# Hash-bucket attention followed by an RWKV channel mix: v centred for all pairs, mix vectors loaded as rows, dummy matmuls in the prologue, one pair's row copies on another queue, and a new instruction order

## The chip, the core and the metric

The kernel runs on one NeuronCore of one Trainium2 chip. The metric is the device time of one launch in microseconds, lower is better. Before the change three runs gave 252.12, 250.82 and 248.18 us, so the median is 250.82 us.

The core has engines that each work through a list of instructions of their own in order: PE (matrix multiply), ACT (activation), DVE (vector), POOL (a slower vector engine) and SP, which here only issues DMAs. ACT issues a few DMAs too. An instruction that waits for a semaphore holds back everything behind it on its engine.

## What is computed

```python
B, H, S, D = 4, 8, 768, 64                      # q, k, v: [B, H, S, D]; proj: [D, 6]
q_bits = (q @ proj) > 0;  k_bits = (k @ proj) > 0       # six sign bits
mask   = all six bits of a query equal those of a key
scores = where(mask, q @ k.T / sqrt(D), -1e9)
attn   = softmax(scores);  o = attn @ v                 # per head
x      = o with heads side by side                      # [B, S, 512]
xk     = x_prev + mu_k * (x - x_prev);  xr the same with mu_r
out    = sigmoid(xr @ w_r) * (relu(xk @ w_k)**2 @ w_v)  # w_k: 512x1024
```

## The kernel before

Two heads make a pair; there are 16 pairs, four to a batch. Each pair `n` goes through these steps.

1. **Load and split.** `ldq` loads q and k (`nat`), `ldv` loads v (`vn`), 384 KB each, on SP's queue. `hi` (L556, or L618 for the first two pairs) rounds four times the value to fp16, `lo` (L559, L621) takes the rest, so that the two fp16 halves stand beside each other in `nh`.
2. **Transpose.** `tr` (L563) is a DMA transpose of `nh` to `a`. For pairs 0 and 1 PE does it instead (L635) and ACT or DVE copies it out of PSUM (`evt`, L639).
3. **Hash bits.** `bits` (L587) multiplies the projection with `a`. A result has six rows for each piece of 256 positions; `GROUPS` says over how many column tiles of PE these are spread (4 unless it is given there, 2 for pairs 1 to 3). `bx` (L591) turns signs into plus or minus a constant, and `row` (L599) copies these rows by DMA behind the 64 rows of the values, so that one matmul gives score plus match bonus. Pair 0 has these rows written directly (L657, L663, L665).
4. **Scores.** Nine steps a pair of 1024 columns: PE L708 into PSUM (three slots of two banks), then ACT L712 takes the exponential into `pt`.
5. **v.** For pairs below `NUC = 8`, v is used as it is: L501 copies it to bf16 with a column of ones (`va`), `vsum` (L509, L512, L515) adds it up, and one extra matmul for each output tile (L736, weights `tiny` = 1e-12) puts in the term that stands for a row without any match. From pair 8 on v is centred: the mean comes from two small matmuls (L528, L529), two instructions of L534 write v minus its mean, and the mean goes into `mc` (L541) and the boundary column (L772).
6. **Output of attention.** PE L741 multiplies `pt` with `va`; DVE takes the reciprocal of the sum (L751, or L753 and L754 where v is centred) and scales (L758, `ob`). The result is turned into `xt` by PE (L794) or by a DMA transpose (L768).
7. **Mix.** L829, L837, L841 make `xk` and `xr` in bf16. L837 multiplies by `muk` or `mur`, and adds `mc` where v is centred.

After the fourth pair of a batch the channel mix of the batch is released: L859 (w_k), `relu` on ACT L864 or DVE L866, the square L869, then L884 (w_r) with a tanh L887, L896 (w_v), L903 and the store L907. So matmuls of batch b fill PE while pairs of batch b+1 wait for ACT.

The order is not found at run time. Each piece of work is recorded with its engine, its dependences and an estimated duration; `ORDER`, a list of 1386 numbers, gives the order in which the recorded pieces are handed to the engines, and `WHERE` gives the engine of each piece that can run on several. A PSUM bank is chosen in that order too. The engines then run their lists in order, and semaphores do the rest. So an entry of `ORDER` decides what stands ahead of what on PE, ACT, DVE, POOL and in SP's DMA queue.

Around this: seven matmuls on zeros (L390) run first, the identity matrices and the weights of `bits` are made on POOL, and `muk` and `mur` are loaded on ACT's queue so that each of 128 partitions gets four values of four bytes:

```python
nc.scalar.dma_start(out=t, in_=src.rearrange("(c p) -> p c", p=P))     # L422, 512 elements of 4 bytes
nc.sync.dma_start(out=a_t[sa][D : D + NB, ...], in_=bx_t[sx][...])     # L599, two or four per pair
```

Of the kernel before, what the change touches and what calls it, by code (L numbers as in the profile page):

```python
# [9 lines left out]
FP32 = mybir.dt.float32  # L10
# [25 lines left out]
def R(kind, n):  # L36
# [223 lines left out]
def kernel(  # L260
# [24 lines left out]
    STEP = 1024  # L285
    NSTEP = 2 * NSC * S // STEP
    NPB = H // 2
    NPAIRS = B * NPB

    NWARM = 7  # L290
    GROUPS = {1: 2, 2: 2, 3: 2}
    HALVED = (2, 3)
    NFOLD = 3
    FW = S // NFOLD
    NUC = 8
    V_GQ = ()
    MERGED = ()
# [667 lines left out]
```

## Time and profile before

| | |
|---|---|
| three runs | 252.12, 250.82, 248.18 us (median 250.82) |
| span of the profiled execution, first to last instruction | 251.3 us |
| PE busy | 236.9 us (94%), 2609 matmuls |
| weight loads of PE | 147.6 us (59%) |
| DVE busy | 195.4 us (78%), 471 instructions |
| ACT busy | 179.1 us (71%), 225 instructions |
| POOL busy | 27.9 us (11%), 73 instructions |
| DMA | 44.56 MB, 177 GB/s on average |

The profile gives no other time for the profiled execution than its span; the span is 0.5 us above the median of the three runs. PE's busy time is modelled for pipelined matmuls, so a busy share of 94% is not 94% of what PE can do. The kernel has four stretches: a prologue up to about 18 us in which PE has little to do; the first batch's attention up to about 60 us; attention and channel mix together up to about 195 us; and the last channel mix up to the end.

### The profile page before, as it was taken

What the parts mean: (1) busy time and instruction counts of PE and PEld (TensorE: products, weight loads), DVE (VectorE), ACT (ScalarE), POOL (GpSimd) and SP (SyncE); (2) the same over time, 40 slices, a digit from 0 to 9 for tenths busy, and PEclk for the clock granted to TensorE, in tenths of its full rate; (3) what the DMA queues carried; (4) which work ended last, traced back from release to release, by engine and by line L of the source; (5) the groups of instructions that cost most, each with busy time, mean ns of one, the idle gap of its engine ahead of it and who ended that gap; (6) DMA issues with size and microseconds to landing.
All of it is one profiled execution on the core that took longest, in us unless ns stands there. A gap on an engine that the chain in (4) does not pass through costs nothing.

```text
span 251.3 us, 6510 instructions
## 1 busy us (share of the span) xinstructions
PE 236.9 (94%) x2609; PEld 147.6 (59%) x2609; DVE 195.4 (78%) x471; ACT 179.1 (71%) x225; POOL 27.9 (11%) x73
## 2 busy tenths in 40 slices
PE   6886799999799998999999999999999999999993
PEld 2444578876566655666467566655865654545442
DVE  3795679889788889898998999899787878376322
ACT  5596689999799978996878899988787223332220
POOL 5002240541302031100001100100000000000000
PEclk9799799999999999999999999999999999999998
DMA  6999999999989999999999996793231030022223
GB/s 187 308 178 251 220 215 191 267 249 189 213 292 241 204 293 292 273 201 269 184 333 186 184 185 158 210 230 57 90 64 44 0 128 28 13 83 86 83 85 125
DMA packets 75194, 44.56 MB, mean 177 GB/s; under 512 B 55524, under 2 KB 70172, under 8 KB 75164
## 3 DMA queue, kind: packets, MB, share of 16 engines
q1 hardware_dynamic: 74028, 44.15, 72.8%
q8 instruction: 20, 0.33, 0.6%
q10 hardware_dynamic: 1136, 0.01, 0.3%
q14 instruction: 10, 0.08, 0.1%
HBM read 24.12 MB, written 6.29 MB: 121 GB/s over the span
## 4 chain that ended last, share of the span: by engine, by line
PE 75%; DMA 11%; DVE 8%; SPq 3%; ACT 1%; issue 1%; DVEq 0%
PE ps_all L708 19%; PE ps_all L896 17%; PE ps_all L859 13%; PE ps_all L741 12%; PE ps_all L884 8%; DMA nat<-in_k_dram 5%; PE ps_all L587 4%; DMA nat<-in_q_dram 3%; DMA a<-bx 2%; DMA os<-in_moe_w_k_dram 1%; DVE nh L559 1%; DVE nh L556 1%; PE ps_all L736 1%; ACT pt L712 1%; PE ps_all L794 1%
## 5 line engine op out<-in xcount | busy, mean ns | idle before, releaser
L712 ACT ACTIVATE pt<-ps_all 128x1024 bf16<-128x1024 f32 x144 | 138.8, 1040 | 21.1 <-PE ps_all L708 19.8
L708 PE MATMUL ps_all<-a 128*128 128x512 f16 (+3 forms) x408 | 80.6, 318 | 5.1 <-DMA a<-bx 3.9
L708 PEld LDWEIGHTS <-a 128*128 128x128 f16 x408 | 35.3, 98 | 26.7 <-DMA a<-bx 4.7
L859 PE MATMUL ps_all<-xk,wk 128*128 128x384 bf16 x256 | 49.0, 326 | 0.9 <-DVE kr L866 0.9
L896 PE MATMUL ps_all<-wv,k 128*128 128x512 bf16 (+1 forms) x200 | 45.9, 370 | 0.6 <-DVE os L903 0.6
L741 PEld LDWEIGHTS <-pt 128*128 128x128 bf16 x1152 | 42.1, 98 | 6.9 <-issue 1.1
L741 PE MATMUL ps_all<-va,pt 128*128 128x65 bf16 x1152 | 43.9, 194 | 0.0
L859 PEld LDWEIGHTS <-wk 128*128 128x128 bf16 x256 | 24.5, 98 | 17.6 <-issue 1.6
L896 PEld LDWEIGHTS <-k 128*128 128x128 bf16 x200 | 19.4, 98 | 20.6 <-issue 0.7
L864 ACT ACTIVATE kr<-ps_all 128x384 bf16<-128x384 f32 x33 | 15.8, 493 | 19.2 <-DVE k L869 12.7
L887 ACT ACTIVATE rs<-ps_all 128x512 f32<-128x512 f32 x24 | 14.2, 603 | 20.9 <-PE ps_all L884 19.0
L559 DVE SCALAR_TENSOR_TENSOR nh<-nat,nh 128x768 f16<-128x768 f32 x28 | 27.3, 976 | 1.1 <-ACT nh L554 0.6
L903 DVE SCALAR_TENSOR_TENSOR os<-rs,ps_all 128x512 f32<-128x512 f32 (+1 forms) x25 | 16.5, 662 | 14.7 <-PE ps_all L896 9.9
L869 DVE TENSOR_TENSOR k<-kr 128x384 bf16<-128x384 bf16 x64 | 21.5, 350 | 3.7 <-ACT kr L864 3.5
L884 PE MATMUL ps_all<-wr,xr 128*128 128x512 bf16 x96 | 23.8, 379 | 0.0
L866 DVE TENSOR_SCALAR kr<-ps_all 128x384 bf16<-128x384 f32 x31 | 17.1, 555 | 8.3 <-PE ps_all L859 6.6
L758 DVE TENSOR_TENSOR ob<-ps_all,rc 128x384 bf16<-128x384 f32 (+1 forms) x36 | 18.3, 511 | 1.0
L884 PEld LDWEIGHTS <-xr 128*128 128x128 bf16 x96 | 9.0, 98 | 10.0 <-ACT kr L864 0.3
L587 PE MATMUL ps_all<-a,p0g 128*32 128x256 f16 (+1 forms) x180 | 13.4, 276 | 1.3 <-DMA a<-nh 1.3
L556 DVE TENSOR_SCALAR nh<-nat 128x768 f16<-128x768 f32 x22 | 12.3, 557 | 3.0 <-DMA nat<-in_q_dram 2.5
L587 PE MATMUL ps_all<-a,p1g 128*32 128x256 f16 (+1 forms) x180 | 12.9, 273 | 0.0
L841 DVE TENSOR_TENSOR xr<-tm,xt 128x768 bf16<-128x768 f16 (+1 forms) x18 | 9.4, 520 | 0.4
(94 smaller groups left out, 187.4 us busy)
## 6 DMA issues: line engine op xcount, KB each, us to landing
vn<-in_v_dram SPq DMA_DIRECT2D x16, 384.0 KB
out_dram<-os SPq DMA_DIRECT2D x23, 256.0 KB
nat<-in_k_dram SPq DMA_DIRECT2D x15, 384.0 KB
nat<-in_q_dram SPq DMA_DIRECT2D x15, 384.0 KB
wst<-in_moe_w_k_dram SPq DMA_DIRECT2D x2, 512.0 KB
wst<-in_moe_w_r_dram SPq DMA_DIRECT2D x2, 512.0 KB
wst<-in_moe_w_v_dram SPq DMA_DIRECT2D x2, 512.0 KB
a<-bx SPq DMA_DIRECT2D x48, 9.0 KB
```

The costliest lines, as they stand in the source:

```text
L559: nc.vector.scalar_tensor_tensor(out=nh[:, :, D:P], in0=nat.rearrange("p j (c d) -> p (j c) d", d=D), scalar=QS, in1=nh[:, :, 0:D], op0=AL ...
L587: nc.tensor.matmul(ps[g_ * wid : (g_ + 1) * wid, 0:FW], w_[:, m_ - 1 - x : m_ - 1 - x + wid], a_t[sa][:, i, x % NFOLD * FW : (x % NFOLD + ...
L708: nc.tensor.matmul(ps[:, lo - s * STEP : hi - s * STEP], side_a["k"][sa][:, j, jc * P : (jc + 1) * P], side_a["q"][sa][:, j, q0 : q0 + hi ...
L712: nc.scalar.activation(out=pt_t[sp][:, s * STEP : (s + 1) * STEP], in_=ps_t[plan.slot[nm]], func=AF.Exp, bias=EBIAS, scale=ESC)
L741: nc.tensor.matmul(oo[:, (ic - c0) * 65 : (ic - c0) * 65 + 65], pt_t[sp][:, o : o + P], va_t[sa][:, j, jc, 0 : D + 1], start=(not uc and i ...
L758: nc.vector.tensor_tensor(out=ob_t[so][:, c0:c1, j * D : (j + 1) * D], in0=oo[:, :, 0:D], in1=rc_t[sr][:, 1, c0:c1].unsqueeze(2).to_broadc ...
L859: nc.tensor.matmul(ps[:, 0:HALF], wk_sb[:, d, fc * P : (fc + 1) * P], xk_t[mx[d]][:, h * HALF : (h + 1) * HALF], start=(d == 0), stop=(d = ...
L866: nc.vector.tensor_scalar(out=kr_t[sk], in0=sm(nm)[:, 0:HALF], scalar1=0.5 ** 0.5, scalar2=0.0, op0=ALU.mult, op1=ALU.max)
L869: nc.vector.tensor_tensor(out=k2_t[s2][:, h * HALF : (h + 1) * HALF], in0=kr_t[sk], in1=kr_t[sk], op=ALU.mult)
L884: nc.tensor.matmul(sm(nr), xr_t[mx[d]][:, c * P : (c + 1) * P], wr_sb[:, d, :], start=(d == 0), stop=(d == NDC - 1))
L896: nc.tensor.matmul(sm(nv)[:, lo:hi], k2_t[(b * NFC + fc) % NK2][:, c * P : (c + 1) * P], wv_sb[:, fc, lo:hi], start=(fc == 0), stop=(fc == ...
L903: nc.vector.scalar_tensor_tensor(out=os_t[so][:, lo:hi], in0=rs_t[s1][:, lo:hi], scalar=1.0, in1=sm(nv)[:, lo:hi], op0=ALU.add, op1=ALU.mult)
```

## The change

- `NUC` goes from 8 to 0: v is centred for all pairs. For pairs 0 to 7 the extra matmuls of L736 and the copies of L501 are gone; the two small matmuls for the mean, the instructions of L534, L541 and L772 and the additional L753 come in.
- `mu_k` and `mu_r` are loaded as eight rows of 128 values, turned by one fp32 matmul with an 8x8 identity (made on POOL), and lowered by one in a single DVE instruction.
- Six more dummy matmuls (`keep`) on the same zeros, placed by `ORDER`; the seven of before are placed anew too.
- The two row copies of pair 1 are issued by ACT (`ROW_ACT`), not by SP.
- `GROUPS` keeps the value 2 for pair 1 alone: `bits` of pairs 2 and 3 are spread over four column tiles, with four row copies each in place of two.
- `ORDER` (now 1429 numbers) and `WHERE` are new throughout.

The core of the diff, without the two tables:

```diff
     NWARM = 7
-    GROUPS = {1: 2, 2: 2, 3: 2}
+    NWARM2 = 6
+    GROUPS = {1: 2}
...
-    NUC = 8
+    NUC = 0
...
-    ROW_ACT = ()
+    ROW_ACT = ((1, 0), (1, 1))
...
-    muk = buf([P, NDC], FP32, "muk")
-    mur = buf([P, NDC], FP32, "mur")
+    mu8 = tm_t[1].bitcast(FP32)[0 : 2 * NDC, 0:P]
+    id8 = buf([2 * NDC, 2 * NDC], FP32, "id8")
+    mu_t = buf([P, 2 * NDC], FP32, "mu")
+    muk, mur = mu_t[:, 0:NDC], mu_t[:, NDC : 2 * NDC]
...
+    for i in range(NWARM2):
+        add("PE", 0.2155, -7.5 + 0.15 * i, lambda: nc.tensor.matmul(sm("warm2"), wz[:, 0:P], wz, start=True, stop=True),
+            r=["wz"], w=["warm2"], ..., name="keep")
...
-    for t, src, key in ((muk, moe_mu_k, "muk"), (mur, moe_mu_r, "mur")):
-        def f_mu(t=t, src=src):
-            with nc.allow_non_contiguous_dma(reason="512 values"):
-                nc.scalar.dma_start(out=t, in_=src.rearrange("(c p) -> p c", p=P))
-        add("ACT", 1.05, -19.0, f_mu, w=[key], ...)
-        add("DVE", 0.17, 1.3, lambda t=t: nc.vector.tensor_scalar(
-            out=t, in0=t, scalar1=-1.0, scalar2=None, op0=ALU.add), r=[key], w=[key])
+    add("POOL", 0.3, -2.2, lambda: make_identity(nc, id8), w=["id8"], name="id8")
+    for i_, src in enumerate((moe_mu_k, moe_mu_r)):
+        add("ACT", 0.42, -19.0, lambda i_=i_, src=src: nc.scalar.dma_start(out=mu8[i_ * NDC : (i_ + 1) * NDC, :], in_=src.rearrange("(c p) -> c p", p=P)),
+            w=[("mu8", i_)], ...)
+    add("PE", 0.12, 1.0, lambda: nc.tensor.matmul(sm("mu")[:, 0 : 2 * NDC], mu8, id8, start=True, stop=True), ...)
+    add("DVE", 0.08, 1.3, lambda: nc.vector.tensor_scalar(out=mu_t, in0=sm("mu")[:, 0 : 2 * NDC], scalar1=-1.0, scalar2=None, op0=ALU.add), ...)
...
-            def row(g_=g_):
-                nc.sync.dma_start(out=a_t[sa][D : D + NB, ...], in_=bx_t[sx][...])
-            add("SP", 0.72, R("row", n) + 0.01 * g_, row, r=[("bx", sx)], ...
+            on = "ACT" if (n, g_) in ROW_ACT else "SP"
+            def row(g_=g_, e=nc.scalar if on == "ACT" else nc.sync):
+                e.dma_start(out=a_t[sa][D : D + NB, ...], in_=bx_t[sx][...])
+            add(on, 0.75, R("row", n) + 0.01 * g_, row, r=[("bx", sx)], ...
```

What the two tables change, counted from the instruction lists of the two programs: of 36 `hi`, DVE has 18 (27 before), ACT 15 (9) and POOL 3 (none); of 64 `relu`, DVE has 24 (31) and ACT 40 (33); of the 16 first sums of `vsum`, DVE has 6 (15) and POOL 10 (1); of the ten weight casts, DVE has 2 (4), ACT 1 (2) and POOL 7 (4). On ACT the two loads of the mix vectors and that of the projection come first, and the activation table is loaded behind them. On SP the loads of v for pairs 1 and 0 come right behind the loads of pair 2. On DVE, `hi` and `lo` of pair 2 stand behind the bits of pair 0's first half (L665) and not ahead of them.

More of the change, by code (lines that the diff above doesn't have):

```diff
@@ L389 @@
     for i in range(NWARM):
-        add("PE", 0.43, -20.0 + 0.1 * i, lambda: nc.tensor.matmul(sm("warm"), wz[:, 0:P], wz, start=True, stop=True),
-            r=["wz"], w=["warm"], take=("sm", "warm", 0) if i == 0 else None, give=["warm"] if i == NWARM - 1 else [])
+        add("PE", 0.2155, -20.0 + 0.1 * i, lambda: nc.tensor.matmul(sm("warm"), wz[:, 0:P], wz, start=True, stop=True),
+            r=["wz"], w=["warm"], take=("sm", "warm", 0) if i == 0 else None, give=["warm"] if i == NWARM - 1 else [], name="warm")
+    for i in range(NWARM2):
+        add("PE", 0.2155, -7.5 + 0.15 * i, lambda: nc.tensor.matmul(sm("warm2"), wz[:, 0:P], wz, start=True, stop=True),
+            r=["wz"], w=["warm2"], take=("sm", "warm2", 0) if i == 0 else None, give=["warm2"] if i == NWARM2 - 1 else [], name="keep")
     add("ACT", 1.5, -9.5, lambda: nc.scalar.activation(out=tb[:, 0:1], in_=tb[:, 1:2], func=AF.Exp), r=["tb"], w=["tb0"], at=0.75, name="table")
@@ L418 @@
                 px[:, 0 : NB * m_].rearrange("p (b f) -> p b f", f=m_)[:, :, m_ - 1], pp[:, 0:NB]), r=[key], w=[(key, g_)], name=f"c{key}{g_}")
-    for t, src, key in ((muk, moe_mu_k, "muk"), (mur, moe_mu_r, "mur")):
-        def f_mu(t=t, src=src):
-            with nc.allow_non_contiguous_dma(reason="512 values"):
-                nc.scalar.dma_start(out=t, in_=src.rearrange("(c p) -> p c", p=P))
-        add("ACT", 1.05, -19.0, f_mu, w=[key], at=0.75, svc=0.2, off=1.5, name=key)
-        add("DVE", 0.17, 1.3, lambda t=t: nc.vector.tensor_scalar(
-            out=t, in0=t, scalar1=-1.0, scalar2=None, op0=ALU.add), r=[key], w=[key])
+    add("POOL", 0.3, -2.2, lambda: make_identity(nc, id8), w=["id8"], name="id8")
+    for i_, src in enumerate((moe_mu_k, moe_mu_r)):
+        add("ACT", 0.42, -19.0, lambda i_=i_, src=src: nc.scalar.dma_start(out=mu8[i_ * NDC : (i_ + 1) * NDC, :], in_=src.rearrange("(c p) -> c p", p=P)),
+            w=[("mu8", i_)], at=0.75, svc=0.05, off=1.5, land=1.05, name=f"ldmu{i_}")
+    add("PE", 0.12, 1.0, lambda: nc.tensor.matmul(sm("mu")[:, 0 : 2 * NDC], mu8, id8, start=True, stop=True),
+        r=["id8", ("mu8", 0), ("mu8", 1)], w=[("mu",)], take=("sm", "mu", 0), name="mu")
+    add("DVE", 0.08, 1.3, lambda: nc.vector.tensor_scalar(out=mu_t, in0=sm("mu")[:, 0 : 2 * NDC], scalar1=-1.0, scalar2=None, op0=ALU.add),
+        r=[("mu",)], w=["muk", "mur"], give=["mu"], name="muv")
     wlist = [("k", c, 1) for c in range(NDC)] + [("r", 0, 2), ("r", 2, 2)] + [("v", c, 2) for c in range(0, NFC, 2)]
@@ L597, in add_bits @@
         for g_ in range(ng):
-            def row(g_=g_):
-                nc.sync.dma_start(out=a_t[sa][D : D + NB, g_ * 4 // ng : (g_ + 1) * 4 // ng, :], in_=bx_t[sx][g_ * wid : g_ * wid + NB * m_, :])
-            add("SP", 0.72, R("row", n) + 0.01 * g_, row, r=[("bx", sx)], w=[("ab", "qk"[i // 2], sa, i % 2, h) for i in range(g_ * 4 // ng, (g_ + 1) * 4 // ng) for h in range(2)],
+            on = "ACT" if (n, g_) in ROW_ACT else "SP"
+            def row(g_=g_, e=nc.scalar if on == "ACT" else nc.sync):
+                e.dma_start(out=a_t[sa][D : D + NB, g_ * 4 // ng : (g_ + 1) * 4 // ng, :], in_=bx_t[sx][g_ * wid : g_ * wid + NB * m_, :])
+            add(on, 0.75, R("row", n) + 0.01 * g_, row, r=[("bx", sx)], w=[("ab", "qk"[i // 2], sa, i % 2, h) for i in range(g_ * 4 // ng, (g_ + 1) * 4 // ng) for h in range(2)],
                 svc={1: 0.3, 2: 0.2, 4: 0.17}[ng], off=1.15, land=1.5, name=f"row{n}")
```

170 rows, old and new, of tables (ORDER, WHERE) are left out of this document.

## The prediction

> **What bounds the kernel now.** I read the table by stretches of time first, then the chain of work that ended last, then the waits, and at the end the groups for prices. In the table the columns behind the stretch are its length, the busy time of PE, PE's weight loads, DVE, ACT and POOL, then PE's granted clock, the DMA share and GB/s.
>
> ```profile
> 18.00:27.00 9.00, 5.09 (x62) 3.40 (x60) 5.66 (x11) 4.98 (x6) 1.67 (x2) 1.00 0.92 256
> 27.00:36.00 9.00, 8.99 (x115) 6.30 (x114) 6.02 (x12) 7.48 (x8) 3.04 (x6) 0.81 1.08 229
> 36.00:60.00 24.00, 24.00 (x437) 19.27 (x437) 20.74 (x56) 23.93 (x27) 6.90 (x14) 1.00 0.98 213
> 60.00:96.00 36.00, 33.39 (x407) 21.19 (x400) 30.49 (x73) 32.36 (x41) 7.05 (x15) 1.00 1.10 247
> 96.00:180.00 84.00, 84.00 (x1055) 53.44 (x1053) 76.49 (x192) 70.92 (x83) 5.16 (x11) 1.00 0.90 208
> 180.00:251.00 71.00, 67.54 (x473) 37.09 (x469) 43.55 (x106) 27.66 (x47) 0.33 (x1) 0.99 0.19 66
> ```
>
> From 96 us on PE never rests: a matmul less there is time less. From 36 to 60 us ACT is full (23.93 of 24), so PE work taken away there is hidden behind the exponentials of L712. Between 18 and 27 us nobody is full: PE has 5.09 of 9. And right behind this hole PE is full at a clock of 0.81. The chain shows what the hole is:
>
> ```profile
> 10.68 0.48 DVE nh L556
> ...
> 11.18 0.96 DVE nh L559
> ...
> 12.17 0.95 DVE a L665
> ...
> 18.45 1.45 PE ps_all L587 x24
> ...
> 20.00 0.42 DVE bx L591
> ...
> 22.07 4.43 DMA a<-bx
> ...
> 26.63 1.70 PE ps_all L708 x7
> ```
>
> The bits of pair 1 end at 19.90, `bx` at 20.42, and then the first score of pair 1 waits for the two row copies until 26.63. The waits put it down to the DMA:
>
> ```profile
> ACT pt L712 <- PE ps_all L708: 4.3, 2, 3.9
> ...
> PE ps_all L708 <- DMA a<-bx: 3.9, 1, 3.9
> ```
>
> ACT loses the same 3.9 us in which it has no scores to work on. The rows are issued from 20.45 on and have landed at 26.50: 6.05 us for two times 18 KB. Ahead of them in SP's queue stand, from 15.62 on, a transpose, a load of v (17.71) and two loads of pair 4 (18.58, 19.09).
>
> **The change, part by part: PE's work.** Prices by columns: a chain row gives 28 matmuls of 384 columns (L859) in 4.55 us, 0.42 ns a column; 48 matmuls of 65 columns (L741) took 1.46 us, 30 ns each.
>
> ```profile
> L736 PE MATMUL ps_all<-vsu,tiny 128*128 128x390 bf16 x12 | 4.4, 365 | 0.3 <-DVE ob L758 0.3
> ...
> L736 PE MATMUL ps_all<-vsu,tiny 128*128 128x195 bf16 x8 | 2.0, 248 | 0.0
> ```
>
> The 20 matmuls of L736 go: 12 x 390 x 0.42 ns + 8 x 195 x 0.42 ns = 2.6 us (the 365 and 248 ns overlap their neighbours). Eight pairs of mean matmuls come: 128 columns 54 ns and one column at most 30 ns, 0.7 us. Bits on two column tiles took 1.43 us (chain, 35.91), on four 0.77 us (51.20): 0.66 us less for each of pairs 2 and 3. The mix matmul has eight columns; I bound it by 30 ns and by four passes, 0.12 us. Together 2.6 - 0.7 + 1.3 - 0.1 = 3.1 us less PE work. What counts: pair 0's part (0.25 us) and pair 3's bits (0.66) lie in 27 to 36, where PE is full, those of pairs 4 to 7 (8 x 0.165 - 4 x 0.085 = 1.0) behind 60, where PE is mostly full. The rest lies beside ACT's 23.93 or in the hole. I take **-2.0 us**, ends -1.0 and -3.1. The six dummies cost at most 6 x 0.43 = 2.6 us (the seven of L390 took 2.97) and lie in PE's idle time of the prologue, where it waits for `lo` (L621); without that cover each that stands ahead of a due transpose costs 0.43. I count nothing, with +0.9 as the bad end.
>
> **The hole.** Four things change it.
> (a) Pair 1's rows leave by ACT, and the new order has two transposes of pair 2 and one 384 KB load still near them in SP's queue, not three loads. A load at 353 GB/s (window 20.0 to 22.4) is 1.1 us, so 2.2 us less stands ahead. The near end is a small DMA on ACT's queue without any load around it:
>
> ```profile
> 0.96 0.59 ACTq L404 DMA_DIRECT2D pj<-in_proj_dram  x1
> ...
> 3.42 0.24 POOL L405 TENSOR_SCALAR npj<-pj 64x6 f32<-64x6 f32 x1 [1.83 <-DMA pj<-in_proj_dram]
> ```
>
> that is 2.46 us from issue to use, which would make the gain 3.6 us; the other end is that nothing is gained.
> (b) The mix vectors no longer go out as 4-byte elements. In the window 22.0 to 24.5, when the rows should move, the profile has
>
> ```profile
> q10 hardware_dynamic: 495, 0.00, 11.1%
> ```
>
> 495 packets on ACT's queue (`muk`, L422, issued at 20.47) that move nothing to speak of: 11.1% of 2.5 us, 0.3 us of all engines. Eight rows of 512 bytes at the start take their place. -0.3.
> (c) On DVE, one `hi` and one `lo` of pair 2 fewer (0.56 + 0.98 us) stand ahead of the copies that end pair 1's transposes; ACT takes the `hi`. The bits of pair 1 start so much earlier at best; ACT's exponentials stand in that chain too (14.73, 1.93 us), so I take -1.2, ends 0 and -1.5.
> (d) The bits of pair 2 and one score step of pair 0, which PE did inside the hole, now stand behind pair 1's first score: 0.77 + 2 x 0.216 = +1.2.
> The sum is **-2.5 us** (-2.5 - 1.2 + 1.2), ends +0.5 and -4.1. ACT now waits for `bx` in its own list before it issues the rows; behind it stand exponentials of pair 0, two issues of 0.37 to 0.59 us are priced in with the 2.46.
>
> **The clock.** 27 to 36 us ran at 0.81 with PE full: 0.19 x 9 = 1.7 us. A gap of 1.2 us before bits near 66 us left the clock at 1.00 from 60 to 96, the gap of 4.2 us did not. With a hole of 1 to 2 us I expect the loss to be gone in most cases: **-1.2 us**, ends 0 and -1.7. The Trainium skill, "TensorE: Matmul & The Clock Gate", section "What's actually happening", says that the clock halves after an idle window of about 3.4 us; by that rule the whole 1.7 us come back as soon as the hole is under it, and the sum would be 0.5 us better.
>
> **DVE, ACT, POOL.** Prices from the groups: L534 550 ns, L753 158, L541 and L772 149. Added on DVE: 16 x 0.550 + 20 x 0.158 + 16 x 0.149 = 14.4 us, all in pairs 0 to 7. Taken off it over the whole run: nine first sums (0.555), nine `hi` (0.56), seven `relu` (0.555), two casts (0.69), two L501 (0.55), small ones, some 17 us. Counted in the new order up to the first score of pair 8, DVE has 3.9 us more than before. It is hidden by DVE's idle time from 36 to 96 us, 3.26 + 5.51 = 8.8 us. ACT gets some 6 us more over the run, up to pair 8 nothing more by the same count; the rest falls behind 96 us, where ACT has 13 us free. POOL takes over ten first sums, and three `hi`, of which the trace has no POOL row: L501 on POOL moves as many elements in 0.93 us, and small copies take up to 2.7 times as long on POOL as on DVE (509 and 186 ns), so 0.9 to 1.5 us; I take 1.2. POOL is busy for a third of its time at most, and pair 4's `hi`, first of them, has until about 45 us. The four row copies in place of two for pairs 2 and 3 cost SP 2 x 2 x 0.75 us of issue, beside its waits of several us. All this: 0, ends -1 and +4.
>
> **The sum.** 251.3 - 2.0 - 2.5 - 1.2 = 245.6 us of span. The profiled span is 0.5 us above the median of the runs, so the time is **245.1 us**. The last 70 us and the store at the end run through the same code and are left alone.
>
> **The rivals.**
> *The hole stays.* Rows issued by ACT run on the same DMA engines and wait for what SP queued before. For it: `muk`, issued on ACT's queue at 20.47, has no packet from 20.0 to 22.4 (all 581 are SP's) and starts when SP's loads run dry. The Trainium skill says so too, "DMA: Bandwidth & Descriptors", section "Issuing engines are not separate DMA queues": another issuing engine saves only issue time. Against it: less stands in the queue at that time. Then only PE's work counts: 251.3 - 2.0 - 0.5 = 248.8 us, within 2%.
> *DVE becomes the bound from 36 to 96 us.* It has 8.8 us free there and gets 14.4 us. If what is taken off DVE lies behind 96 us, 5.6 us don't fit, PE's savings hide behind it, and the hole's gain is eaten by it too: 251.3 + 5.6 - 0.5 = 256.4 us, slower. It decides from a net addition of 8.8 us on; the count says 3.9, unevenly spread, and what runs beside DVE may stretch its instructions (L837 on 768 columns: 417 ns with `muk`, 546 with `mur`).
> *More is gained.* From 60 to 96 us PE has 2.6 us idle, and the chain runs there through DVE pieces that leave (va L501 at 62.47, three vt L509 of 0.49) and DMA landings of 5.9 and 7.2 us. If half of these holes and the whole 1.7 us of clock come back and L736 counts in full: 245.6 - 1.3 - 0.5 - 1.1 - 0.5 = 242.2 us.
>
> **How the numbers follow.** Forecast 0.48 (243.5 to 247.5, three quarters of it under 245.8, the 2% bound, which is also about what a measurement of this kernel can tell from no change), hole stays 0.25, more gained 0.14, DVE bound 0.13. Faster: 0.75 x 0.48 + 0.14 = 0.50, and a third of the first rival, 0.08, for a hole that stays in part while PE's 3.1 us count in full and the clock holds (251.3 - 3.1 - 1.7 - 1.2 - 0.5 = 244.8): 0.58. Slower 0.13. Within 2%: 0.29. The range reaches from below the last rival to above the first, and leaves out the DVE case and a little at each end: 240.5 to 250.5.
>
> **What would show it.** Right: pair 1's first score near 23 us, the wait of L708 for `a<-bx` under 2 us, a clock of 0.95 or more from 24 to 36, no L736, 16 pairs of L528 and L529, PE full behind 96 us as now. Wrong: a wait of 3 us or more for the rows, DVE above 97% from 36 to 90 us with PE and ACT both waiting for it, or PE waiting for L534.

## The result and the profile after

The changed kernel takes 259.46 us (median of four runs, 258.31 to 260.50) against 251.14 for the kernel before on the same chip (248.18 to 252.12): ratio 1.038, 95% interval 1.030 to 1.046. It is slower; the forecast was 245.1, and the range 240.5 to 250.5 does not hold the time. The profiled execution has a span of 257.5 us; the runs lie some 1.8 us above their spans. Times here are medians of all runs, while a ratio and its interval leave out runs that are over 1.5% above the fastest of their kernel, so a ratio can differ a little from the quotient of two medians.

Line numbers have moved by some ten: L708 (scores) is now L719, L712 (exp) L723, L741 (PV) L752, L556 and L559 (`hi`, `lo`) L565 and L568, L587 (bits) L596, L599 (row copies) L610, L534 (centring) L543. The table by stretches of the changed kernel, columns as in the prediction:

```profile
18.00:27.00 9.00, 5.93 (x50) 2.81 (x50) 6.32 (x13) 4.97 (x7) 2.31 (x3) 0.91 0.90 179
27.00:36.00 9.00, 8.72 (x129) 5.74 (x126) 7.08 (x15) 8.01 (x10) 2.59 (x1) 0.90 1.08 243
36.00:60.00 24.00, 19.10 (x326) 14.66 (x324) 17.95 (x56) 19.77 (x22) 7.49 (x12) 1.00 1.06 224
60.00:96.00 36.00, 34.52 (x456) 23.03 (x455) 34.03 (x91) 33.45 (x41) 7.60 (x13) 1.00 1.04 241
96.00:180.00 84.00, 81.79 (x985) 51.00 (x984) 72.67 (x176) 74.54 (x92) 12.45 (x18) 1.00 0.89 201
```

Compare the third row with the one of before. From 36 to 60 us PE was busy for 24.00 us and ACT for 23.93; now 19.10 and 19.77. DVE fell as well, from 20.74 to 17.95. So no engine is full, and a stretch in which two were now has all of them waiting for each other. Not all of it need cost time: e5 below takes as long as the kernel before and has 22.91 and 22.79 there. From 96 to 180 us PE rests for 2.2 us where it never did. The chain that ended last shows both the hole at the start and the new losses:

```profile
19.11 0.42 DVE bx L600
...
20.59 3.86 DMA a<-bx
...
24.50 0.61 PE ps_all L719 x3
...
40.92 0.77 SPq L610
...
41.73 4.75 DMA a<-bx
...
46.53 1.06 PE ps_all L719 x8
...
53.91 1.03 ACT pt L723
54.98 0.53 PE ps_all L752 x12
55.51 0.45 PE ps_all L719 x2
56.03 1.03 ACT pt L723
57.11 0.61 PE ps_all L719 x3
```

The first score of pair 1 starts at 24.50 (before 26.63, forecast near 23). Then, at 40.92, the last two row copies of pair 3 go out, and the scores of pair 3 that need them wait until 46.53. From 53.91 on the chain changes engine with every instruction: an exp, the PV piece that needs this exp, the score behind that PV piece in PE's list, the exp of that score. (PV is the product of `pt` and `va`, L752.) The waits from 36 to 60 us say the same (engine and line, what it waited for, us in total, times, longest):

```profile
ACT pt L723 <- PE ps_all L719: 4.2, 5, 1.4
...
DVE nh L565 <- DMA nat<-in_q_dram: 2.1, 1, 2.1
PE ps_all L719 <- DMA a<-bx: 1.4, 1, 1.4
...
PE ps_all L752 <- ACT pt L723: 1.0, 1, 1.0
PE ps_all L719 <- ACT pt L723: 0.8, 1, 0.8
```

In the profile before neither ACT nor PE has a wait in this stretch: ACT's exponentials run in one piece from 32.40 for 35.28 us.

### The profile page after: what moved, and what is told of

Read it like the earlier page. It is cut to its first block, busy times and chain, and to the rows that moved or that the text cites. A ratio compares the mean times of both kernels' runs of the same rounds, so it can differ in the third digit from the quotient of the medians.

```text
span 257.5 us, 6593 instructions
## 1 busy us (share of the span) xinstructions
PE 237.7 (92%) x2613; PEld 146.3 (57%) x2613; DVE 197.3 (77%) x488; ACT 183.5 (71%) x237; POOL 43.1 (17%) x89
## 4 chain that ended last, share of the span: by engine, by line
PE 66%; DVE 15%; DMA 7%; ACT 5%; issue 3%; SPq 2%; POOL 1%; DVEq 0%; ACTq 0%; POOLq 0%
PE ps_all L719 16%; PE ps_all L907 16%; PE ps_all L870 14%; PE ps_all L752 9%; PE ps_all L895 8%; ACT pt L723 5%; DMA nat<-in_q_dram 4%; DMA a<-bx 3%; PE ps_all L596 3%; DVE nh L568 2%; DVE tm L848 1%; DVE ob L769 1%; DVE nh L565 1%; DVE a L650 1%; DVE kr L877 1%
## 5 line engine op out<-in xcount | busy, mean ns | idle before, releaser
L723 ACT ACTIVATE pt<-ps_all 128x1024 bf16<-128x1024 f32 x144 | 140.0, 1033 | 17.9 <-PE ps_all L719 16.7
L719 PE MATMUL ps_all<-a 128*128 128x256 f16 (+3 forms) x408 | 82.9, 319 | 5.9 <-DMA a<-bx 3.4
L719 PEld LDWEIGHTS <-a 128*128 128x128 f16 x408 | 35.2, 98 | 29.5 <-issue 7.1
L752 PEld LDWEIGHTS <-pt 128*128 128x128 bf16 x1152 | 43.9, 97 | 11.4 <-issue 3.1
L752 PE MATMUL ps_all<-va,pt 128*128 128x65 bf16 x1152 | 46.4, 193 | 2.1 <-ACT pt L723 1.0
L875 ACT ACTIVATE kr<-ps_all 128x384 bf16<-128x384 f32 x40 | 19.1, 493 | 24.2 <-PE ps_all L870 16.8
L880 DVE TENSOR_TENSOR k<-kr 128x384 bf16<-128x384 bf16 x64 | 24.0, 387 | 8.2 <-ACT kr L875 7.9
L568 DVE SCALAR_TENSOR_TENSOR nh<-nat,nh 128x768 f16<-128x768 f32 x28 | 27.7, 997 | 2.4 <-ACT nh L563 2.2
L543 DVE SCALAR_TENSOR_TENSOR va<-ps_all,vn 128x384 bf16<-128x384 f32 x32 | 17.0, 548 | 2.4 <-PE ps_all L538 2.4
L518 POOL TENSOR_TENSOR vt<-vn 128x384 f32<-128x384 f32 x10 | 10.9, 1088 | 47.4 <-DVE df L840 19.1
L848 DVE TENSOR_SCALAR tm<-df,mu,mc 128x768 f16<-128x768 bf16 (+1 forms) x36 | 18.2, 509 | 0.4
L877 DVE TENSOR_SCALAR kr<-ps_all 128x384 bf16<-128x384 f32 x24 | 13.2, 553 | 3.7 <-PE ps_all L870 3.3
L596 PE MATMUL ps_all<-a,p0g 128*32 128x256 f16 (+1 forms) x180 | 12.4, 285 | 1.8 <-DVE ob L769 0.8
```

The source lines that it names most:

```text
L568: nc.vector.scalar_tensor_tensor(out=nh[:, :, D:P], in0=nat.rearrange("p j (c d) -> p (j c) d", d=D), scalar=QS, in1=nh[:, :, 0:D], op0=AL ...
L596: nc.tensor.matmul(ps[g_ * wid : (g_ + 1) * wid, 0:FW], w_[:, m_ - 1 - x : m_ - 1 - x + wid], a_t[sa][:, i, x % NFOLD * FW : (x % NFOLD + ...
L719: nc.tensor.matmul(ps[:, lo - s * STEP : hi - s * STEP], side_a["k"][sa][:, j, jc * P : (jc + 1) * P], side_a["q"][sa][:, j, q0 : q0 + hi ...
L723: nc.scalar.activation(out=pt_t[sp][:, s * STEP : (s + 1) * STEP], in_=ps_t[plan.slot[nm]], func=AF.Exp, bias=EBIAS, scale=ESC)
L752: nc.tensor.matmul(oo[:, (ic - c0) * 65 : (ic - c0) * 65 + 65], pt_t[sp][:, o : o + P], va_t[sa][:, j, jc, 0 : D + 1], start=(not uc and i ...
L848: nc.vector.tensor_scalar(out=flat(tm_t[tm], h0, h1), in0=flat(df_t[sd], h0, h1), scalar1=mu[:, t : t + 1], scalar2=None if n < NUC else m ...
```

## The experiments

The theories: the loss comes from the **new order** of the lists, or from the **parts** (centring, mix rows, split rows). All ratios are against the kernel before, run on the same chip. None of these kernels leaves out a part of the computation.

**The order alone, and the change without the centring.** First (e1) the kernel before with nothing but the new `ORDER` and `WHERE`, then (e2) the changed kernel with v centred from pair 8 on only, as before.

```diff
 e1: NUC = 8; GROUPS = {1: 2, 2: 2, 3: 2}; ROW_ACT = (); NWARM2 = 0; mix vectors as before
 e1: ORDER, WHERE of the changed kernel
 e2: changed kernel with
-    NUC = 0
+    NUC = 8
```

> The new order and engine table with every other part of the change taken back: v uncentred for pairs 0 to 7, mix vectors as 4-byte elements, no additional dummies, pair 1's rows on SP, two row copies for pairs 2 and 3. Order theory (the new list itself loses the time, between 36 and 60 us): 256 to 261 us, at least 5 us above the kernel before. Parts theory (centring, POOL or the four row copies lose it): 247 to 253 us, within 1% of the kernel before.

Measured: 256.31, ratio 1.029 (1.021 to 1.036).

> The changed kernel with v uncentred for pairs 0 to 7, as before; all else as changed. Centring theory (14 us of DVE work, the mean on PE and the wait for v minus mean ahead of the product with v hold PE and ACT up between 36 and 60 us): 251 to 255 us, 4 to 8 us less than the changed kernel. Order theory: 258 to 261 us, no gain, since the 20 small matmuls come back (2 us) while DVE gets freer.

Measured: 254.62, ratio 1.021 (1.018 to 1.024). The order by itself, with its engine table, costs 2.9%, 7 us. Centring costs the difference of the changed kernel to this run, 1.038 - 1.021 = 1.7%, 4 us. The rest of the parts takes 1.029 - 1.021 = 0.8% off, with intervals that overlap. Both theories hold in part. One thing differs besides: the score slots, as e5 below shows.

**Single suspects inside the new order.** Two row copies instead of four for pairs 2 and 3 (e3); the three `hi` that POOL (GpSimd) got back on DVE (VectorE) (e4); other PSUM banks, so that scores of pairs 3 to 5 get three slots (e6); pair 6's q and k loaded earlier (e9); the first, the second and the last of these at once (e17).

```diff
 e3:  GROUPS = {1: 2}                   ->  {1: 2, 2: 2, 3: 2}
 e4:  WHERE: hi4q, hi4k, hi7q  POOL     ->  DVE
 e6:  small tiles, steps 30 to 53: banks 7 and 6 preferred; scores avoid the last two slots
 e9:  SP's list:
 q of pair 5
+q of pair 6
+k of pair 6
 v of pair 4
 v of pair 3
```

> The changed kernel with two row copies and two column tiles for pairs 2 and 3, at the places in SP's queue where the first two of the four stood. Row theory (the last two copies of pair 3 were issued at 40.92 us, 6 us after their bits were ready, behind a transpose and two loads; with them the first score of pair 3 waited until 46.53): first score of pair 3 near 42 us and 255 to 257 us, 3 to 4 us less. Other theories: 258.5 to 260.5, within 1 us of the changed kernel.

> The changed kernel with the three rounding steps of pairs 4 and 7 on DVE (0.55 us each) in place of POOL (2.1 to 2.6 us each). POOL theory (these make the transposes of pair 4 late, which stand in SP's queue ahead of pair 3's rows, and slow DVE beside them): 255 to 257.5 us. Other theories: 258.5 to 261 us, no gain.

> The changed kernel, its order unchanged; only the choice of PSUM banks differs in score steps 30 to 53: small tiles keep to banks 7 and 6 while that costs them no more than about 1 us, scores avoid the slots of the last two steps; 10 instead of 17 of the 24 steps then reuse the slot of two steps earlier. Theory of the slots: 254 to 257.5, that is 2 to 5 us of the loss given back. Theory of the work: 258 to 260.5, as the changed kernel.

> The changed kernel with one thing moved in SP's list: pair 6's q and k loads go out ahead of the v loads of pairs 4 and 3 (near 30 us instead of 40.0 and 44.3). Theory of the loads (the new order fetches v early and q and k late, so that DVE stands 2.15 us at 45.6 for pair 6's q, with pair 4's bits and the ends of pair 3 behind it): the wait goes, 255 to 257.5. Theory of tight order (PE and ACT alternate because score, PV and exp stand next to each other in the new lists): 258 to 260.5.

> The changed kernel with three things taken back at once: two row copies instead of four for pairs 2 and 3, the three scalings of pairs 4 and 7 on VectorE instead of GpSimd, and pair 6's q and k loads ahead of the v loads of pairs 4 and 3. If the waits between 36 and 60 us cover each other (each ends just behind the next): 254 to 257. If the rest of the order holds the time (PV, scores and exps standing next to each other): 258 to 260.5.

Measured: 259.03 (ratio 1.035), 259.11 (1.036), 257.92 (1.031, 1.025 to 1.037), 259.37 (1.036, 1.032 to 1.041), and 261.95 with three undone (1.040, 1.030 to 1.051). No suspect gives the time back, nor do three together. e9 shows how that can be: DVE's wait of 2.1 us for pair 6's q at 45.6 is gone, and an earlier one stands in its place. PE's instructions of e9 (start, length, what ended the idle time before):

```profile
39.04 1.03 PE L719 MATMUL ps_all<-a 128*128 128x128 f16 x8 [1.95 <-DMA a<-bx]
...
55.10 0.53 PE L752 MATMUL ps_all<-va,pt 128*128 128x65 bf16 x12 [0.99 <-ACT pt L723]
57.23 0.59 PE L719 MATMUL ps_all<-a 128*128 128x512 f16 x3 [0.81 <-ACT pt L723]
```

The waits at 55 and 57 us are the ones of the changed kernel, to 0.15 us: what went before them had been caught up or lost elsewhere by then. In e17 ACT's wait for scores from 36 to 60 us has even grown, from 4.2 to 5.3 us.

**Two converses on the kernel before.** Its scores confined to two slots where the changed kernel has in effect two, and pair 6's loads made late.

```diff
 e5:  score steps 30 to 53
+    choices = [c for c in choices if c[2] < 2]
 e10: SP's list:
 k of pair 5
-q of pair 6
+v of pair 3
 ...
 second transpose of pair 4
+q of pair 6
 first transpose of pair 5
+k of pair 6
```

> The kernel before, its order unchanged; only the choice of the score buffers is narrowed: in the 24 score steps of pairs 3 to 5 (numbers 30 to 53) scores may take slots 0 and 1 alone, so that 22 of the 24 reuse the slot of the score step two earlier, as 17 do in the changed kernel and 4 in the kernel before. Theory of the slots (in the changed kernel the small tiles that the order holds open take the third score slot, so that a PV piece between two scores leaves ACT without a score): slower than before by 3 to 6 us, 253 to 256, with ACT idle in 36 to 60 us where it now works 23.9 of 24 us, and groups of waits of about 1 us in which PE waits for an exp and ACT for a score. Theory of the work (the order puts centring and row copies late, the slots are only a trace of that): at most 1 us, 249 to 251.

> The converse on the kernel before: pair 6's q and k loads go out behind pair 4's transposes (near 40 us instead of 30.7 and 35.1), pair 3's v load takes the place of the first. Nothing else moves. Theory of the loads: 2 to 4 us slower than before, 252.5 to 254.5, with DVE waiting for the q load near 45 us. Theory of tight order: within 1 us of before, 249 to 251.5.

Measured: 250.03 with two slots (ratio 1.001, 0.996 to 1.005), so two slots in place of three cost nothing here. One slot was not tried, and that is what the new list gives in e1. The kernel's rule for banks follows the list, and there it puts five scores of pair 3 in a row into the same slot (in e2 and e16 too); the kernel before has no two in a row among pairs 3 to 5, the changed kernel has two (the scores at 55.51 and 57.11). A score then waits for the exp of the score ahead of it, as PE's and ACT's instructions of e1 show:

```profile
50.58 0.60 PE L722 MATMUL ps_all<-a 128*128 128x256 f16 x4 [0.49 <-ACT pt L726]
...
52.35 0.60 PE L722 MATMUL ps_all<-a 128*128 128x256 f16 x4 [0.80 <-ACT pt L726]
...
54.12 0.60 PE L722 MATMUL ps_all<-a 128*128 128x384 f16 x4 [0.90 <-ACT pt L726]
```

```profile
51.28 1.02 ACT L726 ACTIVATE pt<-ps_all 128x1024 bf16<-128x1024 f32 x1 [0.75 <-PE ps_all L722]
53.05 1.02 ACT L726 ACTIVATE pt<-ps_all 128x1024 bf16<-128x1024 f32 x1 [0.74 <-PE ps_all L722]
```

PE waits 2.2 us in these three places. So some of e1's 7 us comes from its slots and is not in the changed kernel; how much, no run shows, and the 1.7% of centring, which is a difference to e2, may be too small for the same reason.

With the late loads 253.13 (1.016, 1.009 to 1.022), 3.9 us: a load that is late for DVE is a cause that exists. The waits of e10 from 36 to 60 us show the whole path:

```profile
DVE nh L556 <- DMA nat<-in_q_dram: 3.1, 1, 3.1
ACT pt L712 <- PE ps_all L708: 3.0, 2, 2.6
PE ps_all L587 <- DVE ob L758: 2.9, 1, 2.9
```

DVE stands 3.1 us before `hi` of pair 6, the end of an earlier pair's output (`ob`) stands behind it in DVE's list, PE's next bits wait 2.9 us for that, and ACT gets no scores for 3.0 us.

**The parts, one at a time, in before's order.** Centring (sums, means, L534, L541 put ahead of each pair's PV); the mix vectors as rows; four column tiles for pairs 2 and 3; mix rows with dummies and pair 1's copies on ACT; and the last again with the two v loads held back that SP would send out in the meantime.

```diff
 e7:  NUC = 8        ->  0
 e11: muk, mur       ->  two loads of rows, id8, mu, muv
 e18: GROUPS = {1: 2, 2: 2, 3: 2}  ->  {1: 2}
 e8:  e11 and ROW_ACT = ((1, 0), (1, 1)), NWARM2 = 6
 e12: e8 and in SP's list
-v of pair 1
-v of pair 2
 first row copy of pair 2
+v of pair 1
+v of pair 2
```

> The kernel before with v centred for all pairs and nothing else of the change: the sums, the means and the centring of pairs 0 to 7 are put into the order of before ahead of each pair's PV, everything else keeps its order. If centring is sound and it was the new order that lost the time: 1 to 3 us below before, 246.5 to 249, with PE's work 2 to 2.6 us less. If centring costs what it cost in the new order (4 to 5 us, by the run with v uncentred), because DVE has to do 3.9 us more up to pair 8: 252.5 to 255.5.

Measured: 253.77, ratio 1.016 (1.009 to 1.022), 3.9 us. In before's order centring costs what it costs in the new one. The stretches 36 to 60 and 60 to 96 us of e7:

```profile
36.00:60.00 24.00, 22.60 (x425) 17.55 (x422) 22.27 (x71) 23.11 (x26) 3.39 (x9) 1.00 1.02 232
60.00:96.00 36.00, 32.99 (x382) 21.07 (x379) 33.82 (x90) 31.80 (x40) 5.92 (x13) 1.00 0.99 245
```

DVE is at 22.27 of 24 and 33.82 of 36 (20.74 and 30.49 before), and PE and ACT are below before in both rows. Over the whole span PE has 1.9 us less to do (235.0 against 236.9) and DVE 9.5 us more (204.9 against 195.4): less work on PE did not make it faster, and more on DVE came with 3.9 us. By which waits is not shown. PE waits 0.7 us for DVE in these two stretches, and this profiled execution (span 250.7) is no longer than that of before. The one long wait that names the centring is earlier: at 22.94 PE has stood 1.47 us for the sum of v, which the matmul of the mean needs. Other places for these instructions in the list were not tried.

> The kernel before with the mix vectors loaded as rows and turned by TensorE, and nothing else: pair 1's two row copies stay on SP's list in their place, no early dummy matmuls. If it was the row copies on the ACT queue that cost the time in the run before (SP's four loads go out 2 us earlier and stand ahead of the copies): 248.5 to 251, as before or up to 1.5 us below. If the vectors as rows cost it (two loads more at the start, a matmul and an identity on POOL): 252 to 255.

> The kernel before with four bit column tiles (and four row copies of half the length) for pairs 2 and 3, and nothing else. By the prediction's steps: 1.3 us less of matmuls on TensorE, against four more issues of 0.75 us on SP, hidden: 248 to 250.5. If SP's list has no room for them: 251 to 254.

> The kernel before with the mix vectors loaded as rows and turned by TensorE, six early dummy matmuls, and pair 1's two row copies on the ACT queue; nothing else of the change, all other instructions in the order of before. By the prediction's steps: the hole behind pair 0 shrinks by 2 to 3 us and the clock of 0.81 goes, 246 to 248. Rival: the landing of the row copies does not move and the copies hold ACT back (two of 0.85 us ahead of three exps), 249 to 251.5.

> The run with mix rows, dummies and pair 1's copies on the ACT queue again, but the two v loads that SP sends out when the copies have left its list are held back behind pair 2's first copy, so that the copies find no more loads ahead of them than in the kernel before. If what stands ahead of the copies sets when they land: landing at or before 26 us and 249 to 251.5. If not (ACT's own time for the two issues, three exps behind them): 253 to 255, as without the hold.

Measured: vectors as rows 249.47 (0.997, 0.994 to 1.001); four tiles 250.89 (1.002, 0.998 to 1.007): neither does anything that can be told from nothing. Mix rows with the copies on ACT 253.91 (1.016, 1.008 to 1.023); with the v loads held back 251.34 (1.007, 1.004 to 1.011). So moving two copies to another engine's queue, with six dummies that were not run apart, cost over 4 us against e11. Holding the loads back gave some 2 us of it back, with intervals that overlap; the traces show how. e8's chain and SP's list, and last a line of SP's list before:

```profile
20.43 0.36 ACTq L609
...
20.83 6.52 DMA a<-bx
...
27.49 2.72 PE ps_all L718 x7
```

```profile
17.36 0.72 SPq L494 DMA_DIRECT2D vn<-in_v_dram  x1
18.18 0.93 SPq L489 DMA_DIRECT2D nat<-in_q_dram  x1
19.16 0.46 SPq L489 DMA_DIRECT2D nat<-in_k_dram  x1
19.67 0.97 SPq L494 DMA_DIRECT2D vn<-in_v_dram  x2
22.99 1.80 SPq L609 DMA_DIRECT2D a<-bx  x2
```

```profile
22.85 0.95 SPq L486 DMA_DIRECT2D vn<-in_v_dram  x2
```

The second copy is in flight from 20.83, 1.24 us earlier than in the profile before (22.07), but takes 6.52 us instead of 4.43 and lands later: SP, freed of the copies, sent two v loads at 19.67 that before went out at 22.85, behind the copies. In e12 the flight takes 4.14 us (20.56 to 24.70). What is left in e12 has a candidate: ACT issues the two copies for 1.6 us, and its exponentials of pair 0 pause for 2.0 us there (2.03 in e8, 2.01 in e12), where e11 runs them in one piece.

**The order cut in time.** The operations of the kernel before throughout; one part of the list in before's order, the rest in the new one, with the engines of `WHERE` accordingly.

```diff
 e13: ORDER = first 200 of before, rest as in the changed kernel's order   (cut near 40 us)
 e14: first 500 of before, rest new                                        (near 80 us)
 e15: first 225 new, rest as before                                        (near 42 us)
 e16: first 450 new, rest as before                                        (near 77 us)
```

> The operations of the kernel before; the first 200 of the written-out order (23 score steps, to about 40 us) in before's order, everything behind in the new order. If the loss of the order alone (6 to 7 us) sits between 40 and 80 us: 253 to 256. If it is made at the start: 249.5 to 251.5. If behind 80 us: 255 to 257.

> The same with the first 500 of the order (63 score steps, to about 80 us) in before's order and the rest in the new one. Loss between 40 and 80 us, or at the start: 249.5 to 251.5. Loss behind 80 us: 253 to 257.

> The converse: the first 225 (25 score steps, to about 42 us) in the new order, the rest in before's. Loss at the start: 253 to 256. Loss behind 40 us: 249.5 to 252.

> The first 450 (56 score steps, to about 77 us) in the new order, the rest in before's. Loss at the start or between 40 and 80 us: 254 to 257. Loss behind 80 us: 249.5 to 252.

Measured: 255.70 (1.028, 1.020 to 1.037), 254.42 (1.022, 1.015 to 1.029), 256.05 (1.027, 1.017 to 1.037), 256.27 (1.029, 1.022 to 1.037). Each mixture loses 5 to 7 us, about as much as the whole new order, so the losses do not add up. In e14 the largest wait sits right behind the cut: up to 86.18 us PE waits 3.2 us for row copies that come late there. The waits of e14 from 70 to 90 us:

```profile
DVE bx L776 <- ACT pt L897: 3.4, 1, 3.4
PE ps_all L893 <- DMA a<-bx: 3.2, 1, 3.2
ACT pt L897 <- PE ps_all L893: 2.5, 3, 1.7
```

So this run says something of the seam, not of the new order behind 80 us. The exponentials say more of the place. There are nine to a pair, and they run nearly in the order of the pairs; these are the starts of the 10th, the 28th and the 37th in the profiles, in us:

| | 10th | 28th | 37th | 28th to 37th | span |
|---|---|---|---|---|---|
| before | 27.3 | 45.2 | 53.7 | 8.5 | 251.3 |
| two slots (e5) | 24.7 | 41.7 | 50.9 | 9.2 | 248.5 |
| new order to 42 us (e15) | 28.8 | 48.9 | 57.9 | 9.0 | 255.6 |
| order alone (e1) | 29.9 | 48.6 | 59.6 | 11.0 | 257.0 |
| changed | 27.0 | 45.2 | 57.7 | 12.5 | 257.5 |

From the 28th to the 37th all runs with before's list in this stretch take 8.2 to 9.5 us (e10, with its late loads, 11.4), all ten with the new list 10.6 to 15.6. So one place is common to them, the scores of pair 3 between about 42 and 60 us, and in the changed kernel it holds 4.0 us of the 6.2 between the two spans. e15 shows another ahead of 49 us. **What in the lists** makes the new order lose there is **not settled**: late loads can do it (e10), yet undoing one such wait brings another forward (e9), and one slot taken five times in a row does it in e1. That an order without these waits loses nothing was not tried.

## Why the prediction was wrong

**PE's work, -2.0: the edits came as priced, the time did not.** No L736 is left, the means are there as 16 pairs of matmuls, PE is at full clock behind 96 us. But the four tiles alone change nothing (e18), and centring alone, which takes 1.9 us off PE, costs 3.9 us (e7). What a matmul less is worth had been read from a PE column at 8.99 of 9 and 84.00 of 84; in the changed kernel this column is at 8.72 and 81.79, so PE waits where it was taken to be full.

**The start of the sum, 251.3 - 0.5.** The 64 runs of the kernel before whose spans are on record lie 1.81 to 1.98 us above them. By that the profiled 251.3 belongs to a run of some 253.1 to 253.3 us, longer than any of the 68 measured (246.47 to 252.81), and 245.6 us of span would have been a run of 247.4. The sum set out from an unusually long execution and took 0.5 off where some 1.8 had to be added.

**The hole, -2.5, and the clock, -1.2: sized on one execution.** In the profiles, the first score came 2.1 us earlier (24.50 against 26.63), and the wait of PE for the copies fell from 3.9 to 1.5 us, under the mark of 2 us that the prediction set. Yet kernels with before's list, unchanged up to 30 us, show what that is worth. Two of them, e5 and e14, with the same instructions in the same order up to there (PE waiting for pair 1's copies):

```profile
PE ps_all L713 <- DMA a<-bx: 1.5, 1, 1.5
```

```profile
PE ps_all L893 <- DMA a<-bx: 4.1, 1, 4.1
```

Of five profiles with this list, two have the wait of 3.9 to 4.1 us and a clock of 0.81 to 0.83 from 27 to 36 us (before, e14), three have 0.8 to 1.5 us and a clock of 1.00 (e5, e10, e13). In e5 the first score of pair 1 starts at 24.03, ahead of the changed kernel's 24.50, and the span is 248.5. The 4.2 us hole that carried 3.7 of the forecast's 5.7 us was one outcome of several, and the runs of before are wide enough to hold both. The ends of this step, +0.5 and -4.1, were added up wrongly too: its parts give +0.9 and -4.2. Part (a) of that step was also too kind: e8 shows that rows on ACT's queue wait for SP's loads like all others. The Trainium skill, "DMA: Bandwidth & Descriptors", section "Issuing engines are not separate DMA queues", says that another issuing engine only saves issue time; e8's row agrees, and shows that it may do harm (6.52 us in flight against 4.43).

The clock did not come back with the short wait either: 0.91 and 0.90 in the first two rows after, where the forecast wanted 0.95 or more. That is 0.09 x 9 + 0.10 x 9 = 1.7 us, as much as the 0.19 x 9 of before, so in these profiles the term of -1.2 was nothing. (The gap near 66 us that the prediction gives as 1.2 is one of PE's weight loads; PE itself stood 1.00 us there.) In the changed kernel PE waits three times within 5 us, and the clock falls behind the last (window from 24 to 30 us):

```profile
19.59 0.48 PE L668 MATMUL ps_all<-a,p 128*32 128x384 f16 x2 [0.88 <-DVE bx L600]
...
22.44 0.59 PE L719 MATMUL ps_all<-a 128*128 128x256 f16 x3 [0.61 <-ACT pt L723]
...
24.50 0.61 PE L719 MATMUL ps_all<-a 128*128 128x512 f16 x3 [1.46 <-DMA a<-bx]
```

```profile
24.00:27.00 3.00, 2.50 (x31) 1.26 (x31) 0.56 (x1) 2.08 (x4) 0.00 (x0) 0.74 1.00 223
27.00:30.00 3.00, 3.00 (x47) 2.03 (x44) 2.87 (x7) 2.06 (x4) 0.00 (x0) 0.69 1.14 279
```

**DVE, ACT, POOL, 0: the part that was priced wrong.** It counted the added work net of what is taken off (3.9 us more on DVE up to pair 8) and let it vanish in idle time of 8.8 us, spread over 60 us. Centring costs 4 us in either order (e7, and the changed kernel against e2). That this is the 3.9 of the count is chance: centring adds 9.5 us to DVE in e7 and 11.1 in the new order (186.2 in e2, 197.3 after). DVE stays under the 97% that the rival of a full DVE set (34.03 of 36 after), and fell from 36 to 60, so this rival's time of 256.4 comes near without its mechanism. The upper end of +4 for this step was about the true value of it. Smaller terms: `hi` on POOL took 2.13 and 2.59 us, not 1.2, and cost nothing all the same (e4); the split row copies, priced as hidden, were (e18 alone, e3 undone).

**The new order had no term at all: the step that failed most.** It was taken as a carrier of the parts, with a price only where a part was moved. By itself it costs 2.9% (e1, its slots included), more than any part. Neither the forecast nor a rival had it: PE and ACT waiting for each other with no engine full was not among the four. From run to run, in ratios, the order makes +2.9%, mix rows, dummies, ACT's copies and four tiles -0.8%, centring +1.7%. That this gives the measured 3.8% is no test, since each is the difference to the run ahead of it. And the prices hold for their list alone: in before's order mix rows, dummies and ACT's copies cost 1.6% (e8).

No kernel of the study is faster than before beyond its interval; the vectors as rows alone come nearest (0.997, 0.994 to 1.001).

## What to carry to other kernels

Price a new order of the same work as a change of its own, by running it alone: here it cost 2.9%, more than any part. Look then at what else follows from the list, as the PSUM slots did here. Idle time of an engine need not take up new work for nothing: 9.5 us more on DVE cost 3.9 us, though DVE had 8.8 us free in the stretch where it was to be hidden. A wait read from one execution may be gone in the next: here one list gave 3.9 or 4.1 us in two executions and 0.8 to 1.5 in three, so look at a second one before sizing a gain on it. When a transfer moves to another queue, look at what the old queue now sends earlier; it may stand ahead of the very transfer that was to be sped up.

## What the runs showed of the hardware

- The same instructions up to 30 us gave a wait of 0.8 to 1.5 us for two small copies in three executions and of 3.9 to 4.1 us in two, with the clock at 1.00 or at 0.81 to 0.83 behind it.
- The granted clock fell to 0.74 and 0.69 with no wait of PE over 1.46 us (three within 5 us), and to 0.58 from 24 to 27 us behind a single wait of 2.31 us (e11); a single wait of 1.48 us left it at 1.00 (e5). The Trainium skill, "TensorE: Matmul & The Clock Gate", section "What's actually happening", puts the drop behind an idle window of about 3.4 us; these rows have it earlier.
- GpSimd (POOL) took 2.13 to 2.59 us for a scaling of 128x768 from fp32 to fp16 for which VectorE takes 0.57.
- On VectorE, `lo` (L568) took up to 1.64 us against a median of 0.96 in the first 60 us of the changed kernel; at 16.24 us it took 1.48 while sums ran on GpSimd.
